# Attention times values with the values stationary in four column tiles, its result turned on VectorE, a job queue per engine and score steps in halves: a two-layer transformer on one core

## The chip, the cores and the metric

The kernel runs on one core of a Trainium2 chip. The metric is device time in microseconds of one execution of the whole program, as a median of several runs. Beside it there is one profiled execution, with its own time; the span in a profile runs from its first to its last instruction. TensorE (PE) multiplies matrices, with a row of its own for loading the stationary operand (PEld); VectorE (DVE), ScalarE (ACT) and GpSimd (POOL) work on elements; SyncE (SP) issues DMAs.

## The reference

Two layers, each an attention with a compressive memory (A) and a gated FFN (B), on 2,048 tokens of width 512; both layers use the same weights.

```python
x = x + A(layernorm(x)); x = x + B(layernorm(x))      # twice
# A: 32 heads of 16, 4 segments of 512 tokens, one after another
for s in range(4):
    logits = einsum('bhqd,bhkd->bhqk', qs, ks) * scale + mask      # causal inside the segment
    a_dot = einsum('bhqk,bhkd->bhqd', softmax(logits), vs)
    a_mem = (phi(qs) @ M) / (phi(qs) @ z + 1e-6)                   # phi(t) = t + 1 if t > 0 else exp(t)
    o = g * a_mem + (1 - g) * a_dot                                # g = sigmoid(beta), per head
    M, z = M + phi(ks)^T vs, z + sum(phi(ks))
# A ends in o @ wo;  B: (gelu(x @ w_gate) * (x @ w_up)) @ w_down, inner width 1792
```

## The kernel before

**Stages.** The work is 8 blocks k = 0..7 (layer k // 4, segment s = k % 4). Class `Att` makes for each block q, kf and kB transposed (feature b*128.. in partitions, token along the row), v by tokens (`vaug`: 16 columns a head and a 17th that holds 1 + exp(beta), so that one product gives numerator and denominator), scores, their product with v, and the memory's part (`mem_items`, `upd_item`). Class `Ffn` holds the output projection (`wo`), gate, up and down. kB is kf with every other head's 16 rows set to zero (`maskB`): a score matmul takes 16 rows of kf for even heads (par 0) or 32 rows of kB for odd ones.

**Scores.** A block has 20 score steps (`STEPS`): for each of four groups b of eight heads there are five steps, in which four row tiles of TensorE (32 rows each) write two PSUM tiles `st` of 128 keys x 1,024. ACT turns each into `pt` = exp(scale * st) by one instruction (L578), POOL zeroes the upper triangle of the diagonal blocks (`affine_select`, L592).

**Flush.** After steps 2 and 4 of a group the probabilities of four heads and all four key blocks are there and a flush follows: 64 in all. For each of 10 pairs of key block and query block and each head, pt (128 keys x 128 queries) is the stationary operand and 17 columns of vaug stream:

```python
nc.tensor.matmul(ps()[:, qi, j, :], lhsT=two[j // 2][:, j % 2, cb:cb + P],
                 rhs=self.vaug[:, ki, 8 * b + 2 * j + par, :], start=(c == 0), stop=(c == len(order) - 1))
```

That is 40 matmuls and 40 weight loads; the result `ps_q` has queries in partitions. DVE takes the reciprocal of the 17th column (L619) and multiplies (L628) into `ab`; behind the second flush of a group it adds the memory's part `am` (L644, blocks with s > 0), and a transposing DMA (`turn`, L215) makes aT, the stationary side of the output projection.

**Order.** Nothing runs by itself: Python plans the program with one clock per engine (`Clocks`) and writes each instruction into its engine's queue as the plan reaches it. The loop at the end follows TensorE's clock: a score step goes first when its operands and both `st` tiles are free, then the matmuls of the item that is open (an `Item`: a list of matmuls with a due time, one or more PSUM banks of four), then the ready item with the earliest due time; if a bank is free and nothing is ready, a filler matmul on a constant tile (`warm_ps`, L853). When an item's last matmul is planned, its function `done` writes the work of the other engines that follows at once: `evict` (L311 ff.) picks DVE or ACT by which clock would be done first, with `ACT_EVICT` in favour of DVE. The scheduled engines take their queues strictly in this order. kB is made by POOL (L382) behind the eviction of kf.

Of the kernel before, what the change touches and what calls it, by code (L numbers as in the profile page):

```python
# [21 lines left out]
NSEG = 4  # L22
L = 512
# [4 lines left out]
TPS = L // P  # L28
SCALE = DH ** -0.5
# [6 lines left out]
BY_PE = {("xnTf", 0), ("xnTf", 2 * NSEG - 1)}  # L36
# [7 lines left out]
ACT_EVICT = 0.5  # L44
FIRST_EVICT = 2.0


class Clocks:
# [5 lines left out]
    LATENCY = 0.055  # L54
    OVERLAP = {"act": 0.09, "dve": 0.07}

    def __init__(self):
        self.pe = self.act = self.dve = self.pool = self.sp = 0.0
        self.table = "exp"
        self.later, self.seq = [], 0  # L60
        self.ev = {}
# [8 lines left out]
    def run_due(self, t):  # L70
        while self.later and self.later[0][0] <= t:
            heapq.heappop(self.later)[2]()

    def run(self, engine, ready, *costs):

        for cost in costs:
            start = max(getattr(self, engine), ready + self.LATENCY)
            ready = start + cost
            setattr(self, engine, ready - self.OVERLAP.get(engine, 0.0))
        return ready  # L80

    def on_act(self, ready, cost, table=None):
        if table and table != self.table:
            self.act += 1.28
            self.table = table
        return self.run("act", ready, cost)
# [9 lines left out]

class Item:


    def __init__(self, due, ready, ops, done=None, banks=1, kind=""):  # L100
        self.due, self.ready, self.ops, self.done, self.banks, self.kind = due, ready, ops, done, banks, kind
# [3 lines left out]
def kernel(  # L105
# [56 lines left out]
    for h in range(2):  # L162
        pieces.append((64.0 + 5.0 * h, lambda h=h: load(
            wd_sb[:, 7 * h:7 * h + 7, :], B_w_down.rearrange("(ft p) n -> p ft n", p=P)[:, 7 * h:7 * h + 7, :])))
# [4 lines left out]
    warm_ps = psp.tile([P, L], F32, tag="m", bufs=M_BANKS)  # L169
# [26 lines left out]
    vaugs = [cst.tile([P, TPS, H, DH + 1], BF16, name=f"vaug{i}") for i in range(SETS)]  # L196
# [6 lines left out]
    def late_constants():  # L203
        for va in vaugs:
            nc.gpsimd.tensor_copy(out=va[:, :, :, DH], in_=cden[:].unsqueeze(1).to_broadcast([P, TPS, H]))
        for b in range(4):
# [5 lines left out]
    def turn_later(t, out, in_, landed):  # L212

        def go():
            nc.sync.dma_start_transpose(out=out, in_=in_)  # L215
            landed(ck.run("sp", t, 1.25) + 1.4)

        ck.at(t, go)


    class Norm:
        def __init__(self, key, tt0, bufs):
            self.key, self.tt0, self.bufs, self.mv = key, tt0, bufs, None
            self.n = 0

        def stats(self, j, ready):
            if self.mv is None:
                self.mv = wrk.tile([P, TPS, 2], F32, tag="bnmv", bufs=3)
            st6 = wrk.tile([P, 1, 6], F32, tag="bnst", bufs=4)
            nc.vector.bn_stats(out=st6[:, 0, :], in_=x_sb[:, self.tt0 + j, :])  # L230
            nc.vector.bn_aggr(out=self.mv[:, j, :], in_=st6[:])
            t = ck.run("dve", ready, 0.66, 0.17)
            self.n += 1
            if self.n == TPS:
                ck.at(t, lambda: self.scales(t))

        def scales(self, ready):
            ve = wrk.tile([P, TPS, 1], F32, tag="lnve")
            nc.gpsimd.tensor_scalar(out=ve[:], in0=self.mv[:, :, 1:2], scalar1=EPS_LN, scalar2=None, op0=ALU.add)
            self.rs = wrk.tile([P, TPS, 1], F32, tag="lnrs", bufs=3)  # L240
            nc.gpsimd.tensor_tensor(out=self.rs[:], in0=ve[:], in1=mhalf[:], op=ALU.pow)  # L241
            t = ck.run("pool", ready, 0.25, 1.05)
            if self.key in BY_PE:
                self.items_by_pe(t)
            else:
                ck.at(t, lambda: self.turned(t))

        def normed(self, j):
            xn = seg.tile([P, D], BF16, tag="xn", bufs=6)
# [4 lines left out]
        def turned(self, ready, j=0):  # L254
            if j == 0:
                self.xnT = seg.tile([P, KT, L], BF16, tag=self.key[0], bufs=self.bufs)
            xn = self.normed(j)
            t = ck.run("dve", ready, 0.333)

            def landed(t2):  # L260
                if j < TPS - 1:
                    self.turned(t, j + 1)
                else:
                    ev[self.key] = t2

            turn_later(t, self.xnT[:, :, j * P:(j + 1) * P], xn[:], landed)

        def items_by_pe(self, ready):
            self.xnT = seg.tile([P, KT, L], BF16, tag=self.key[0], bufs=self.bufs)
            left = [TPS]  # L270

            def item(j):
                xn = self.normed(j)
                t = ck.run("dve", ready, 0.333)
                ps = Box(lambda: psp.tile([P, KT, P], BF16, tag="m", bufs=M_BANKS, name="ps"))

                def done():
                    t2 = evict(self.xnT[:, :, j * P:(j + 1) * P], ps()[:])
                    left[0] -= 1
                    if not left[0]:  # L280
                        ev[self.key] = t2

                return Item(-0.5, lambda: t + Clocks.LATENCY <= ck.pe,
                            [(Clocks.MM[128], lambda kt=kt: nc.tensor.transpose(
                                ps()[:, kt, :], xn[:, kt * P:(kt + 1) * P], ident[:])) for kt in range(KT)],
                            done, kind="turn")

            ck.at(ready, lambda: items.extend([item(j) for j in range(TPS)]))

        def by_pe(self, j):  # L290
            xn = self.normed(j)
            ps = psp.tile([P, KT, P], BF16, tag="m", bufs=M_BANKS)
# [8 lines left out]

    banks = [0.0] * M_BANKS

    def product(name):
        return Box(lambda: psp.tile([P, L], F32, tag="m", bufs=M_BANKS, name=name))

    def free_bank(t):
        banks.append(t + 0.05)
        banks.sort()

    def evict(dst, src):  # L311
        ready = ck.made()
        on_dve = max(ck.dve, ready) + 0.67
        on_act = max(ck.act, ready) + 0.6
# [15 lines left out]
    class Box:  # L330
        def __init__(self, make):
            self.make, self.t = make, None
# [11 lines left out]
    class Att:  # L344
# [202 lines left out]
        def scores(self, t):  # L547
            k = self.k
            b, i = divmod(t, PAIRS)
            if i == 0:  # L550
                self.pts = {}
# [338 lines left out]
```

## Time and profile before

| | us |
|---|---|
| median of 3 runs | 599.21 (599.03 to 600.44) |
| the profiled execution's own time | 598.08 |
| its span | 596.2 |
| exponentials of scores, ACT, 320 | 310.1 |
| masks, POOL, 448 | 196.7 |
| gate, up and down matmuls, each 448 (busy time, overlapping) | 106.3, 102.6, 103.5 |

A line of a group reads: line, engine, operation, out<-in, shape, count, then busy time and mean duration in ns, then the idle time of the engine just ahead of them and what ended it. In the chain of waits, a piece has its start, its length and who ran. A window's row gives the busy time of PE, PEld, DVE, ACT and POOL, the granted clock (1.00 is full speed), the DMA share and GB/s. "issue" is idle time that no wait explains. Some matmul records are missing from the trace, so its counts can fall short of the program's.

### The profile page before, as it was taken

The numbers are of one execution on the slowest core, as the hardware profiler recorded it, in microseconds if no ns is written. First come the engines' busy times: TensorE is split into PE (matmuls) and PEld (weight loads), VectorE is DVE, ScalarE is ACT, GpSimd is POOL, SyncE is SP. The second block draws the span as 40 slices with busy tenths as digits, with TensorE's granted clock in tenths as the row PEclk, the third lists the DMA queues.
The fourth block names the chain that finished last, engine by engine and source line by source line (L and its number), as shares of the span: only waits on it lengthen the run. The fifth ranks groups of instructions, "written<-read, shape, count | busy, mean of one in ns | idle before, by whom it ended". The sixth has DMA issues, their size and how long they took to land.

```text
span 596.2 us, 14275 instructions
## 1 busy us (share of the span) xinstructions
PE 571.8 (96%) x5759; PEld 279.8 (47%) x5844; DVE 455.5 (76%) x921; ACT 415.2 (70%) x442; POOL 270.9 (45%) x527
## 2 busy tenths in 40 slices
PE   8898899999999999999999999999999999999997
PEld 3344444454445444444445455444454455444443
DVE  7889979776987777886677898789777885868161
ACT  2678779788868877897679957797478936770410
POOL 4777757433553356544546435553346424410000
PEclk9999979899999999999999999999999999999999
DMA  6178460200041002301230013200230003200001
GB/s 212 28 145 241 94 151 11 46 10 10 3 76 23 1 11 54 63 10 20 46 54 12 1 36 63 37 10 10 57 60 18 3 9 56 35 12 18 19 0 35
DMA packets 68513, 26.88 MB, mean 45 GB/s; under 512 B 59488, under 2 KB 67424, under 8 KB 68448
## 3 DMA queue, kind: packets, MB, share of 16 engines
q1 hardware_dynamic: 68304, 25.97, 20.5%
q8 instruction: 45, 0.74, 0.5%
q14 instruction: 20, 0.16, 0.1%
q10 hardware_dynamic: 144, 0.01, 0.0%
HBM read 9.71 MB, written 2.10 MB: 20 GB/s over the span
## 4 chain that ended last, share of the span: by engine, by line
PE 77%; DVE 13%; POOL 3%; issue 3%; ACT 2%; DMA 2%; ACTq 0%
PE psg L326 17%; PE psd L326 16%; PE psu L326 14%; PE ps_q L612 9%; PE st L571 7%; PE psqk L326 5%; PE pso L326 4%; PE psv L326 2%; DVE st L230 2%; POOL kB L382 2%; DVE xn L250 1%; PE warm_ps L853 1%; ACT pt L578 1%; DVE e L427 1%; POOL pt L592 1%
## 5 line engine op out<-in xcount | busy, mean ns | idle before, releaser
L578 ACT ACTIVATE pt<-st 128x1024 bf16<-128x1024 f32 x320 | 310.1, 1021 | 117.0 <-PE st L571 114.7
L592 POOL TENSOR_SCALAR_AFFINE_SELECT pt<-pt 128x256 bf16<-128x256 bf16 (+1 forms) x448 | 196.7, 459 | 214.6 <-ACT pt L578 208.0
L326 PE MATMUL psg<-xnT,wg_sb 128*128 128x512 bf16 x420 | 106.3, 382 | 3.3 <-DMA xnT<-xn 1.1
L326 PE MATMUL psd<-wd_sb,gel 128*128 128x512 bf16 x430 | 103.5, 380 | 2.0 <-DVE gel L705 0.9
L326 PE MATMUL psu<-xnT,wu_sb 128*128 128x512 bf16 x432 | 102.6, 379 | 0.8
L705 DVE TENSOR_TENSOR gel<-gel,psu 128x512 bf16<-128x512 bf16 x112 | 75.5, 685 | 31.2 <-PE psu L326 28.8
L612 PEld LDWEIGHTS <-pt 128*128 128x128 bf16 x2560 | 74.6, 96 | 21.1 <-issue 5.4
L612 PE MATMUL ps_q<-vaug,pt 128*128 128x17 bf16 x2560 | 76.3, 171 | 4.4 <-POOL pt L592 3.2
L319 DVE CAST gel<-psg 128x512 bf16<-128x512 f32 x96 | 64.8, 685 | 18.2 <-PE psg L326 17.0
L382 POOL TENSOR_SCALAR kB<-kf,maskB 128x512 bf16<-128x512 bf16 x32 | 50.5, 1579 | 35.3 <-DVE kf L319 31.6
L326 PEld LDWEIGHTS <-wu_sb 128*128 128x128 bf16 x448 | 41.8, 98 | 50.6 <-issue 4.3
L326 PEld LDWEIGHTS <-gel 128*128 128x128 bf16 x448 | 40.7, 98 | 51.2 <-issue 8.6
L326 PEld LDWEIGHTS <-wg_sb 128*128 128x128 bf16 x448 | 39.0, 98 | 49.0 <-issue 11.5
L719 DVE TENSOR_TENSOR x_sb<-x_sb,psd 128x512 bf16<-128x512 bf16 x32 | 21.9, 685 | 43.4 <-PE psd L326 43.4
L736 ACT ACTIVATE gel<-gel 128x2048 bf16<-128x2048 bf16 (+1 forms) x28 | 45.2, 1684 | 0.1
L230 DVE BATCH_NORM_STATS2 st<-x_sb 128x6 f32<-128x512 bf16 x60 | 41.4, 690 | 1.7
L571 PE MATMUL st<-q,kf 16*128 16x128 bf16 (+3 forms) x512 | 35.3, 306 | 1.1
L326 PE MATMUL psqk<-xnT,wq_sb 128*128 128x512 bf16 x123 | 34.7, 388 | 1.0 <-DVE xnT L297 0.6
L571 PE MATMUL st<-q,kB 32*128 32x384 bf16 (+3 forms) x512 | 34.5, 300 | 1.0
L326 PE MATMUL psqk<-xnT,wk_sb 128*128 128x512 bf16 x122 | 34.3, 388 | 0.5 <-issue 0.2
L326 PE MATMUL pso<-wo_sb,aT 128*128 128x512 bf16 x122 | 30.5, 379 | 0.8 <-DVE gel L705 0.4
L250 DVE TENSOR_SCALAR xn<-x_sb,mv,rs 128x512 bf16<-128x512 bf16 x64 | 29.7, 494 | 1.8 <-POOL rs L241 1.6
(82 smaller groups left out, 508.3 us busy)
## 6 DMA issues: line engine op xcount, KB each, us to landing
out_dram<-x_sb SPq DMA_DIRECT2D x16, 128.0 KB, 1.7
wg_sb<-in_B_w_gate_dram SPq DMA_DIRECT2D x4, 448.0 KB, 4.2
wu_sb<-in_B_w_up_dram SPq DMA_DIRECT2D x4, 448.0 KB, 6.5
wd_sb<-in_B_w_down_dram SPq DMA_DIRECT2D x2, 896.0 KB, 6.2
x_sb<-in_A_x_dram SPq DMA_DIRECT2D x3, 512.0 KB, 8.5
xnT<-xn SPq DMA_TRANSPOSE x52, 2.5
x_sb<-in_A_x_dram SPq DMA_DIRECT2D x4, 128.0 KB, 2.9
wq_sb<-in_A_wq_dram SPq DMA_DIRECT2D x1, 512.0 KB, 5.7
```

The lines of the kernel that those rows point to most:

```text
L230: nc.vector.bn_stats(out=st6[:, 0, :], in_=x_sb[:, self.tt0 + j, :])
L250: nc.vector.tensor_scalar(out=xn[:], in0=x_sb[:, self.tt0 + j, :], scalar1=self.mv[:, j, 0:1], scalar2=self.rs[:, j, :], op0=ALU.subtract, ...
L319: nc.vector.tensor_copy(out=dst, in_=src)
L326: return [(Clocks.MM[512], lambda i=i, l=l, r=r: nc.tensor.matmul(ps()[:], lhsT=l(), rhs=r(), start=(i == 0), stop=(i == n - 1))) for i, ( ...
L382: nc.gpsimd.tensor_scalar(out=self.kB[:, b, :], in0=self.kf[:, b, :], scalar1=maskB[:, 0:1], scalar2=None, op0=ALU.mult)
L571: nc.tensor.matmul(sts[j // 2][:, j % 2, c0:c0 + N], lhsT=lhsT[rows, b, P * ki:P * ki + P], rhs=self.q[rows, b, P * ki:L], start=True, sto ...
L578: nc.scalar.activation(out=pt[:], in_=st[:], func=ACT.Exp, scale=SCALE)
L592: nc.gpsimd.affine_select(out=dv, in_=dv, pattern=[[0, w], [1, P]], compare_op=ALU.is_ge, fill=0.0, base=0, channel_multiplier=-1)
L612: nc.tensor.matmul(ps()[:, qi, j, :], lhsT=two[j // 2][:, j % 2, cb:cb + P], rhs=self.vaug[:, ki, 8 * b + 2 * j + par, :], start=(c == 0), ...
L705: nc.vector.tensor_tensor(out=g, in0=g, in1=ps()[:], op=ALU.mult)
L719: nc.vector.tensor_tensor(out=xt, in0=xt, in1=ps()[:], op=ALU.add)
L736: nc.scalar.activation(out=g, in_=g, func=ACT.Gelu_apprx_tanh)
```

## The change

1. **Flush.** vaug is now the stationary operand: for each key block, 32 columns of vaug (a head's 17 and the 15 that follow, which nothing reads) in each of four column tiles, one a head, and the probabilities of all later queries stream (512, 384, 256 or 128 columns). 16 matmuls in place of 40. The result has head j in partitions 32j.., with queries along the row.
2. **Turn.** DVE transposes that tile in blocks of 32x32 into `byq` (f32, SBUF), takes reciprocal and product as before into `ab`, and behind the second flush transposes `ab` in 32x32 blocks into aT. The memory's part goes through the transposing DMA instead (`amT`) and is added to aT.
3. **Job queues.** Each engine has a queue of jobs (`Engine`), with a time from which a job may start and a slack; `serve` writes the job whose time plus slack is lowest. An eviction is posted to DVE and ACT at once, and whichever comes to it first takes it. Buffers are named one by one (`m0` to `m3`, `xn0` to `xn3`, `st0`, `st1`) instead of taken from rotating pools.
4. **Half steps.** A score step can be issued as two halves with two row tiles and one `st` tile each, where TensorE has nothing else to do. A flush that is ready goes right behind a score step.
5. kB is made by DVE; the w_down loads come later and in four pieces; POOL also zeroes the 15 columns behind vaug's last head.

```diff
+class Engine:
+    def serve(self, now):
...
+        start = max(self.free, min(j[0] for j in self.jobs) + self.LATENCY)
+        if start > now:
+            return False
+        job = min((j for j in self.jobs if j[0] + self.LATENCY <= start + 0.03), key=lambda j: j[0] + j[1])
...
-    for h in range(2):
-        pieces.append((64.0 + 5.0 * h, lambda h=h: load(
...
+    for h in range(4):
+        r = slice(FT * h // 4, FT * (h + 1) // 4)
+        pieces.append((94.0 + 3.2 * h, lambda r=r: load(
...
-                nc.gpsimd.tensor_scalar(out=self.kB[:, b, :], in0=self.kf[:, b, :], scalar1=maskB[:, 0:1],
-                                        scalar2=None, op0=ALU.mult)
...
+                    ck.dve.post(t, NORMAL, (0.285, lambda: nc.vector.tensor_scalar(
+                        out=self.kB[:, b, :], in0=self.kf[:, b, :], scalar1=maskB[:, 0:1], scalar2=None,
+                        op0=ALU.mult), lambda t2: ev.update({("kB", k, b): t2})))
...
-        def scores(self, t):
+        def scores(self, t, halves):
...
-                for j in range(4):
+                for j in [2 * n + m for n in halves for m in range(2)]:
...
         def flush_item(self, b, par, pts, masked):
             k = self.k
-            ps = Box(lambda: psp.tile([P, TPS, 4, DH + 1], F32, tag="m", bufs=M_BANKS, name="ps_q"))
...
-                nc.tensor.matmul(ps()[:, qi, j, :], lhsT=two[j // 2][:, j % 2, cb:cb + P],
-                                 rhs=self.vaug[:, ki, 8 * b + 2 * j + par, :], start=(c == 0),
-                                 stop=(c == len(order) - 1))
+            ps = Psum()
+            order = (0, 1, 3, 2) if par == 0 else (0, 2, 1, 3)
...
+                for n, ki in enumerate(order):
+                    two, c0 = pts[par, ki]
+                    for j in range(4):
+                        h = 8 * b + 2 * j + par
+                        nc.tensor.matmul(ps()[32 * j:32 * j + 32, P * ki:L],
+                                         lhsT=self.vaug[:, ki, h * (DH + 1):h * (DH + 1) + 32],
+                                         rhs=two[j // 2][:, j % 2, c0:c0 + L - P * ki], start=(n == 0), stop=(n == 3),
+                                         tile_position=(0, 32 * j))
...
+                def turn():
+                    made["byq"] = byq = wrk.tile([P, TPS * 4, 32], F32, tag="byq", bufs=1, name="byq")
+                    nc.vector.transpose(out=byq[:].rearrange("p a c -> p (a c)"), in_=ps()[:])
...
+                def back():
...
+                    nc.vector.transpose(out=self.aT[:, b, :], in_=self.ab[b][:].rearrange("p a c -> p (a c)"))
+
+                def add():
+                    nc.vector.tensor_tensor(out=self.aT[:, b, :], in0=self.aT[:, b, :], in1=self.amT[b][:], op=ALU.add)
...
+                ck.dve.post(ck.made(), SOON, (0.673, turn, ps.read), (0.251, inverse, None),
+                            (0.417, scale, kept if par else None))
...
+        free = [f <= ck.pe - 0.05 for f in st_free]
+        if half:
+            return (1,) if free[1] else ()
+        return (0, 1) if all(free) else (0,) if free[0] and idle else ()
```

TensorE's queue around the first flush (block 0; `st` are scores, `warm` fillers, `pt` probabilities). Before, the end of the fifth score step, fillers, and the flush's first pair:

```order
L571 MATMUL st<-q,kB 128x128
L853 LDWEIGHTS warm
L853 MATMUL warm_ps<-warm 128x512
L853 LDWEIGHTS warm
L853 MATMUL warm_ps<-warm 128x512
L612 LDWEIGHTS pt
L612 MATMUL ps_q<-vaug_131,pt 128x17
```

And with the change (`m` is a PSUM bank):

```order
L1044 LDWEIGHTS warm
L1044 MATMUL m<-warm 128x512
L710 LDWEIGHTS kB
L710 MATMUL st<-q,kB 128x384
L710 LDWEIGHTS kB
L710 MATMUL st<-q,kB 128x384
L710 LDWEIGHTS kB
L710 MATMUL st<-q,kB 128x128
L710 LDWEIGHTS kB
L710 MATMUL st<-q,kB 128x128
L756 LDWEIGHTS vaug_131
L756 MATMUL m<-pt,vaug_131 32x512
```

Of the fifth score step only one half (two row tiles) stands ahead of the flush, and its other half behind; the flush holds vaug and streams pt in 32 rows of output.

DVE's queue over the first two flushes of block 0 (`st_` are statistics of the next norm, `xn` its normalized rows). Before:

```order
L619 RECIPROCAL r<-ps_q 128x16
L628 TENSOR_TENSOR ab<-ps_q,r 128x16x16
L619 RECIPROCAL r<-ps_q 128x16
L628 TENSOR_TENSOR ab<-ps_q,r 128x16x16
L250 TENSOR_SCALAR xn<-x_sb,mv,rs 128x512
L425 TENSOR_SCALAR e<-e 128x512
L427 SCALAR_TENSOR_TENSOR e,zk<-kf,e 128x512
```

With the change:

```order
L769 STREAM_TRANSPOSE byq<-m 128x512
L773 RECIPROCAL r<-byq 128x16
L778 TENSOR_TENSOR ab<-byq,r 128x16x16
L784 STREAM_TRANSPOSE aT<-ab 128x512
L339 CAST kf<-m 128x512
L395 TENSOR_SCALAR xn<-x_sb,mv,rs 128x512 x4
L486 TENSOR_SCALAR kB<-kf,maskB 128x512 x2
L555 TENSOR_SCALAR e<-e 128x512
L541 SCALAR_TENSOR_TENSOR e,zk<-kf,e 128x512
```

The second flush of the group is followed by two transposes in place of one DMA, and two kB multiplications that POOL did stand between xn and the next phi.

More of the change, by code (lines that the diff above doesn't have):

```diff
@@ L22 @@
 NSEG = 4
+NK = 2 * NSEG
 L = 512
@@ L68, in at, with when, serve, busy @@
         heapq.heappush(self.later, (t, self.seq, fn))
[L70 to L86, printed above, removed]
+    def when(self, cond, fn):
+        if cond():
+            fn()
+        else:
+            self.waiting.append((cond, fn))
+    def serve(self):
+        again = True
+        while again:
+            again = False
+            while self.later and self.later[0][0] <= self.pe:
+                heapq.heappop(self.later)[2]()
+                again = True
+            for w in list(self.waiting):
+                if w[0]():
+                    self.waiting.remove(w)
+                    w[1]()
+                    again = True
+            first = min(self.engines, key=lambda e: max(e.free, min((j[0] for j in e.jobs), default=1e9)))
+            again |= first.serve(self.pe) or any(e.serve(self.pe) for e in self.engines)
+    def busy(self):
+        return self.later or self.waiting or any(e.jobs for e in self.engines)
     def made(self):
@@ new lines, in evict, with end, dense @@
+    def evict(ps, dst, src, told, slack=NORMAL):
+        taken = []
+        def end(t):
+            ps.read(t)
+            told(t)
+        first = FIRST_EVICT if ("scores", 0) not in ev else ACT_EVICT
+        ck.dve.post(ck.made(), slack, (0.673, lambda: nc.vector.tensor_copy(out=dst(), in_=src()), end), taken=taken)
+        ck.act.post(ck.made(), slack + first, (0.602, lambda: nc.scalar.activation(
+            out=dst(), in_=src(), func=ACT.Copy), end), taken=taken)
+    def dense(ps, pairs):
+        n = len(pairs)
+        return [(Clocks.MM[512], lambda i=i, l=l, r=r: nc.tensor.matmul(ps()[:], lhsT=l(), rhs=r(), start=(i == 0),
+                                                                        stop=(i == n - 1)))
+                for i, (l, r) in enumerate(pairs)]
@@ new lines, with next_e @@
+    streams = [(k, t) for k in range(NK) for t in range(STEPS)]
+    opened, half = None, 0
+    def next_e():
+        if not e_slots.free or e_slots.queue:
+            return
+        now = streams[0][0] + streams[0][1] / STEPS if streams else 1e9
+        act = ck.act
+        idle = act.free <= ck.pe and act.table == "exp" and not any(j[0] <= ck.pe and not j[4] for j in act.jobs)
+        got = [j for j in e_jobs if j[1] <= ck.pe and j[2]() and (idle or j[0] <= now)]
+        if got:
+            job = min(got, key=lambda j: j[0])
+            e_jobs.remove(job)
+            job[3](job[1], E_SLACK)
+            ck.serve()
@@ new lines, in score_now, with open_item @@
+    def score_now(idle=False):
+        if not streams or not (step_free or half):
+            return ()
+        k, t = streams[0]
+        if not att[k].score_ready(t):
+            return ()
+        free = [f <= ck.pe - 0.05 for f in st_free]
+        if half:
+            return (1,) if free[1] else ()
+        return (0, 1) if all(free) else (0,) if free[0] and idle else ()
+    def open_item(got):
+        it = min(got, key=lambda it: it.due)
+        items.remove(it)
+        it.ps.bank = min((i for i in range(M_BANKS)), key=lambda i: banks[i])
+        banks[it.ps.bank] = 1e9
+        return it
@@ new lines, in score @@
+    def score(halves):
+        k, t = streams[0]
+        att[k].scores(t, halves)
+        if halves[-1]:
+            streams.pop(0)
+        got = [it for it in items if it.kind == "flush" and it.ready()]
+        if got and min(banks) <= ck.pe:
+            it = open_item(got)
+            it.ops[0][1]()
+            ck.on_pe(it.ops[0][0] - Clocks.SWITCH)
+            it.done()
+        return 1 - halves[-1]
+    while streams or items or opened or ck.busy():
+        ck.serve()
+        next_e()
+        halves = score_now()
+        if halves:
+            half = score(halves)
```

753 lines of the change are left out of this document (396 added, 357 removed).

## The prediction

> **What bounds the kernel now.** I read the page first: busy shares, the slices, the chain of waits.
>
> ```profile
> span 596.2 us, 14275 instructions
> PE 571.8 (96%) x5759; PEld 279.8 (47%) x5844; DVE 455.5 (76%) x921; ACT 415.2 (70%) x442; POOL 270.9 (45%) x527
> PEclk9999979899999999999999999999999999999999
> PE 77%; DVE 13%; POOL 3%; issue 3%; ACT 2%; DMA 2%; ACTq 0%
> ```
>
> The reader is to see that TensorE is busy in 96% of the span at full clock, except for two slices early on, and that 77% of the chain that ended last is TensorE itself. DVE has 24% idle, ACT 30%. So time is TensorE's queue, and a change is worth what it takes out of that queue, unless another engine makes TensorE wait. A busy PE row overlaps its neighbour, so I price TensorE from start to start, in the chain of waits and in the timeline of stage 218 to 232 us:
>
> ```profile
> 546.25 4.53 PE psd L326 x21
> 592.77 0.69 DVE x_sb L719
> 222.98 2.11 PE L326 MATMUL psd<-wd_sb,gel 128*128 128x512 bf16 x9 [0.16 <-issue]
> 225.02 0.40 PE L571 MATMUL st<-q,kB 32*128 32x512 bf16 x4
> 225.35 0.82 PE L326 MATMUL psd<-wd_sb,gel 128*128 128x512 bf16 x3
> 226.01 1.15 PE L612 MATMUL ps_q<-vaug,pt 128*128 128x17 bf16 x40
> 227.01 0.81 PE L326 MATMUL psd<-wd_sb,gel 128*128 128x512 bf16 x2
> ```
>
> A dense matmul of 512 columns costs 4.53 / 21 = 0.216 us. Nine of them from 222.98 end their turn at 224.92; the score step begins at 225.02 and the next dense matmul at 225.35. A **score step** thus costs 0.43: 0.10 to enter, 0.216 for four row tiles of 512 columns that stream together, 0.11 to leave. A **flush** (40 matmuls of 17 columns, in the whole array) costs 227.01 - 226.01 = 1.00, nothing to enter or leave.
>
> Only the first 105 us are not like this. The first q matmul and the first gate matmul in the timeline, and the busy time by stretches of 20 us (PE, PEld, DVE, ACT, POOL, clock):
>
> ```profile
> 10.39 1.02 PE L326 MATMUL psqk<-xnT,wq_sb 128*128 128x512 bf16 x4 [0.61 <-DVE xnT L297]
> 105.81 0.61 PE L326 MATMUL psg<-xnT,wg_sb 128*128 128x512 bf16 x1
> 40.00:60.00 20.00, 17.94 (x200) 9.08 (x200) 19.02 (x43) 16.02 (x20) 15.85 (x24) 1.00 0.77 222
> 60.00:80.00 20.00, 17.23 (x221) 8.43 (x222) 16.04 (x38) 14.66 (x19) 12.24 (x24) 0.79 0.61 137
> 80.00:100.00 20.00, 19.67 (x212) 9.58 (x214) 18.43 (x41) 16.60 (x22) 12.74 (x22) 0.95 0.26 53
> 540.00:560.00 20.00, 19.74 (x102) 9.47 (x104) 11.42 (x23) 2.91 (x6) 1.27 (x2) 1.00 0.08 26
> 560.00:580.00 20.00, 19.95 (x93) 9.10 (x93) 8.36 (x13) 6.54 (x11) 0.00 (x0) 1.00 0.00 1
> 580.00:600.00 20.00, 12.63 (x58) 5.56 (x57) 4.02 (x6) 0.00 (x0) 0.00 (x0) 0.97 0.08 26
> ```
>
> TensorE's order before the first gate matmul holds 208 dense matmuls (44.9), 31 score steps (13.3), 11 flushes (11.0), 30 fillers (6.5) and 100 small ones (68 of 128 columns, 32 of 8, at a quarter and an eighth of 0.216: 4.6); with 10.4 ahead of them that is 90.7. The gate came at 105.8: **15 us of waiting and of slow clock** in the start. There DVE is busy 18 or 19 of 20 us. The end, by the same sum, loses only some 10 us more in the 487 us that follow.
>
> **The change part by part.** The groups whose counts change:
>
> ```profile
> L612 PE MATMUL ps_q<-vaug,pt 128*128 128x17 bf16 x2560 | 76.3, 171 | 4.4 <-POOL pt L592 3.2
> L853 PE MATMUL warm_ps<-warm 128*128 128x512 bf16 x49 | 16.0, 419 | 1.0 <-DVE vaug L319 0.6 <-DVE am L475 0.2
> L319 DVE CAST gel<-psg 128x512 bf16<-128x512 f32 x96 | 64.8, 685 | 18.2 <-PE psg L326 17.0
> L425 DVE TENSOR_SCALAR e<-e 128x512 bf16<-128x512 bf16 x48 | 16.3, 341 | 1.7 <-ACT e L421 1.6
> L427 DVE SCALAR_TENSOR_TENSOR e<-kf,e 128x512 bf16<-128x512 bf16 x24 | 17.9, 746 | 0.8
> L382 POOL TENSOR_SCALAR kB<-kf,maskB 128x512 bf16<-128x512 bf16 x32 | 50.5, 1579 | 35.3 <-DVE kf L319 31.6
> L316 ACT ACTIVATE kf<-psqk 128x512 bf16<-128x512 f32 x4 | 2.4, 598 | 0.4 <-PE psqk L326 0.4
> ```
>
> *Flushes.* There are 64. Each becomes 16 matmuls: for four key blocks of 512, 384, 256 and 128 columns, four column tiles side by side. If the four stream together, as the four row tiles of a score step do, that is 1,280 columns at 0.216 / 512, or 0.54, with 0.10 to enter and 0.11 to leave: 0.75. 64 x (0.75 - 1.00) = **-16.0**. No row shows column tiles; the bounds are 0.54 (no entry, no exit) and 0.75 + 0.40, where weights are not hidden (rival A). I take 0.75, since entry and exit are measured on the nearest row.
>
> *Neighbours.* In the new order 12 flushes stand right behind a score step and 16 right ahead of one; there one entry and exit are shared instead of two: 28 x -0.10 = **-2.8** (bounds 0 and -2.8).
>
> *Half steps.* 20 of the 160 score steps are issued as two halves with two row tiles each. A half streams the same columns, so it costs a whole 0.43 more: 20 x 0.43 = **+8.6**. They stand among fillers, where TensorE has nothing else; the fillers rise from 49 to 58: 9 x 0.216 = **+1.9**. Half steps and fillers are idle time made visible: the faster flushes leave TensorE ahead of ACT in the early stages.
>
> *What DVE takes over.* 64 turns of a 128x512 f32 tile out of PSUM, 32 turns of a 128x512 bf16 tile, 32 kB multiplications. DVE rows with 512 elements in a partition lie between 0.341 (bf16, one source) and 0.746; a turn reads PSUM like the cast, so I take 0.685. kB is like the row at 0.341. 96 x 0.685 + 32 x 0.341 = 76.7. The order hands 58 evictions from DVE to ACT (gate 35, k 9, v 8, q 6): -58 x 0.685 = -39.7. DVE: 455.5 + 37 = 492.5, of some 585 us 84%. ACT takes 58 x 0.60 = 35 and stands at 450, 77%. POOL loses all 50.5 of kB. The bank of a flush is held as long as before (0.685, against reciprocal 0.25 and product 0.42). All this lies beside TensorE, as long as DVE's queue doesn't grow: its cover is the 24% idle. If it is gone, each turn shows (rival B).
>
> Bounds for a turn: 0.341 below; above, two passes over the tile, 1.37. The page "VectorE: DVE Perf Modes" of the Trainium skill (The three transpose paths) gives 311 ns for a 128x128 bf16 turn in 32x32 blocks; with 384 more elements at its 0.96 GHz an estimate is 0.71, by which the DVE sum would be 2 us higher and the time the same.
>
> *Transposing DMAs.* 32 DMAs of ab become 24 of am, which has long been there when it is needed; output projection no longer waits for a DMA behind the last flush. No row of the waits names an output projection that waited for it, so I count 0 there. The loads of w_down go out later in four pieces; their first use is 30 us and more behind, also 0.
>
> *Start.* In the new order 85.2 us of TensorE stand before the first gate matmul (208 dense 44.9, 34 score steps 14.6, 10 flushes 7.5, 26 fillers 5.6, small ones 2.2, and 10.4). kB, on the chain in this stage, goes from 1.58 to about 0.34:
>
> ```profile
> 17.48 1.57 POOL kB L382
> 19.77 1.54 POOL kB L382
> 35.33 1.79 POOL kB L382
> 38.43 1.54 POOL kB L382
> ```
>
> ACT now has 58 exponentials at 1.02, 11 of phi at 0.63 and 30 evictions and copies at 0.60 ahead of the first gate eviction, 84 us behind the 9.8 at which it starts, some less since neighbours overlap. So the gate can hardly come before 90; I expect 97, a loss of 12 in place of 15: **-3**. The bounds are -10 (ACT packed) and +3 (as much lost as before, and DVE's turns in front).
>
> **Sum**, against the profiled execution's own 598.1 (span 596.2): -16.0 - 2.8 + 8.6 + 1.9 - 3 = -11.3, so 586.8. The median before, 599.21, lies 1.1 above that execution: **588**.
>
> **The rivals.**
>
> *A: weights of the column tiles aren't hidden (slower).* A flush loads 16 sets of weights. Where a set must wait for the stream ahead of it, four loads show at each of four key blocks. Rows of a score step, loads and matmuls:
>
> ```profile
> 222.42 0.10 PEld L571 LDWEIGHTS <-kf 16*128 16x128 bf16 x4 [0.23 <-issue]
> 222.43 0.29 PE L571 MATMUL st<-q,kf 16*128 16x256 bf16 x4
> 222.44 0.10 PEld L571 LDWEIGHTS <-kB 32*128 32x128 bf16 x4
> 222.55 0.28 PE L571 MATMUL st<-q,kB 32*128 32x256 bf16 x4
> ...
> L326 PEld LDWEIGHTS <-gel 128*128 128x128 bf16 x448 | 40.7, 98 | 51.2 <-issue 8.6
> ```
>
> Four loads take 0.10, so the price is 4 x 0.10 = 0.40 a flush: 64 x 0.40 = +25.6, or 613. It turns slower from 0.18 a flush on. Against it: kB's loads lie inside the stream of kf's matmuls on the same rows. The page "TensorE: Matmul & The Clock Gate" of the Trainium skill (Part 3, The mechanism) says that loads overlap running matmuls only where the row group differs, and all column tiles share the row groups; by that rule this rival would be the forecast. The rows above speak against the rule, and so do the loads of gel, 0.098 each on all rows of the array, which fit into the 0.216 rhythm of the dense matmuls. Chance 8%.
>
> *B: a turn takes two passes (slower).* 96 x 0.685 = +66, so DVE has 558 to do; with the 32 us that it can't use at the end (11.4, 8.4 and 4.0 busy from 540 to 596) and 8 at the start it can't end before 598, with waits about 606. Chance 9%.
>
> *C: more gain.* The start packs against ACT (-7 more) and entry and exit of a flush overlap (0.65, -6): 575. Chance 10%.
>
> *D: no change.* DVE at 84%, one queue in order, answers later; TensorE waits for banks:
>
> ```profile
> PE ps_q L612 <- POOL pt L592: 3.2, 7, 0.8
> PE psg L326 <- DVE am L475: 0.4, 1, 0.4
> ```
>
> Such waits are small now. 0.17 us at each of 64 flushes returns it all: 597 to 601. Chance 10%.
>
> *E: the column tiles run one behind another,* so the change doesn't do what it says: 4 x 0.54 + 0.21 = 2.37 a flush, +104 on the sum, 692. The four row tiles, together in 0.40, speak against it. Chance 3%.
>
> **How the numbers follow.** The forecast itself (578 to 597) has 60%. 574 to 604 leaves out the lower part of C (4%), A, E and half of B, some 19%. What a measurement of this kernel can tell from no change is 0.3%, 1.8 us. Faster: the forecast, C, and a little of D, 0.72; the same, 0.09; slower: A, B, E, the edge of D, and of the start's loss, 0.19.
>
> **What would show it.** In the profile after: from a flush's first matmul to the next dense one 0.65 (with 0.10 ahead of it); 16 loads inside the flush without a gap; turns at 0.69; DVE near 490, ACT near 450, POOL near 220 busy; the first gate matmul near 97; no PE wait of over 5 us in total on DVE. The forecast is wrong if flushes cost 0.93 or more, if turns are 1.0 or more, or if TensorE's rows show new idle on DVE or ACT.

## The result, and the profile after

| | before | changed |
|---|---|---|
| median, measured side by side | 599.83 us (599.03 to 601.18, 4 runs) | 582.81 us (581.52 to 585.5, 4 runs) |
| the profiled execution's own time | 598.08 | 584.07 |
| its span | 596.2 | 582.4 |

The ratio is 0.972, with a 95% interval of 0.9675 to 0.9765: 17 us faster. The forecast was 588, so the sign and the range held and the point was 5 us too high.

The page of the changed kernel: its span, busy times, the granted clock in 40 slices, and the engines' shares of the chain of waits.

```profile
span 582.4 us, 11265 instructions
PE 559.6 (96%) x4240; PEld 234.2 (40%) x4317; DVE 484.5 (83%) x991; ACT 441.7 (76%) x500; POOL 226.0 (39%) x498
PEclk8999999999999999999999999999999999999999
PE 75%; DVE 16%; DMA 3%; issue 3%; ACT 2%; POOL 0%; POOLq 0%; another core or an unknown queue 0%; DVEq 0%; ACTq 0%
```

TensorE is as busy as before (96%) in a span 13.8 us shorter: it still bounds, and what went is work in its queue and the gaps of the start. DVE has 29 us more to do, ACT 26 more, POOL 45 less.

The timeline of TensorE in the same stage as before (start, length, instruction, count, in brackets the idle time ahead), first a flush that adjoins a score step, then one between dense matmuls:

```profile
207.67 2.33 PE L345 MATMUL m<-wd_sb,gel 128*128 128x512 bf16 x10
209.93 0.40 PE L710 MATMUL st<-q,kf 16*128 16x384 bf16 x8
210.26 0.73 PE L756 MATMUL m<-pt,vaug 128*32 128x512 bf16 x16
210.92 1.69 PE L345 MATMUL m<-wd_sb,gel 128*128 128x512 bf16 x6
...
234.78 1.47 PE L345 MATMUL m<-xnT,wg_sb 128*128 128x512 bf16 x6
236.18 0.73 PE L756 MATMUL m<-pt,vaug 128*32 128x512 bf16 x16
236.84 0.39 PE L345 MATMUL m<-xnT,wg_sb 128*128 128x512 bf16 x1
```

The second: six dense matmuls from 234.78 end their turn at 234.78 + 6 x 0.216 = 236.08; the flush begins 0.10 to 0.11 later and the next dense matmul 0.66 after that. A flush alone is **0.77**, where it was 1.00. The first: ten dense matmuls end at 209.83 and the next begins at 210.92, so a score step and a flush side by side take 1.09, where apart they take 0.43 + 0.77 = 1.20: one exit and entry are shared, worth 0.11.

The groups that are new or grew (out<-in, shape, count, busy us, mean ns, idle ahead and what ended it):

```profile
L769 DVE STREAM_TRANSPOSE byq<-m 128x512 f32<-128x512 f32 x64 | 45.3, 707 | 11.2 <-PE m L756 10.8
L784 DVE STREAM_TRANSPOSE aT<-ab 128x512 bf16<-128x512 bf16 x32 | 22.6, 706 | 0.6
L486 DVE TENSOR_SCALAR kB<-kf,maskB 128x512 bf16<-128x512 bf16 x32 | 11.6, 369 | 0.7 <-ACT kf L340 0.5
L340 ACT ACTIVATE gel<-m 128x512 bf16<-128x512 f32 x37 | 21.7, 603 | 21.2 <-PE m L345 20.4
```

A turn takes 0.707 whether it is f32 out of PSUM or bf16 out of SBUF, and ACT now evicts 37 gate tiles, where it evicted 2.

The start, by the timeline and by stretches of 20 us (PE, PEld, DVE, ACT, POOL, clock), and TensorE's longest waits and the last eviction:

```profile
10.81 1.59 PE L345 MATMUL m<-xnT,wq_sb 128*128 128x512 bf16 x4 [0.61 <-DVE xnT L431]
90.08 1.89 PE L345 MATMUL m<-xnT,wg_sb 128*128 128x512 bf16 x7
578.84 0.69 DVE L820 TENSOR_TENSOR x_sb<-x_sb,m 128x512 bf16<-128x512 bf16 x1 [2.33 <-PE m L345]
```

```profile
0.00:20.00 20.00, 16.18 (x77) 6.56 (x79) 13.05 (x35) 8.03 (x13) 8.11 (x25) 0.91 0.48 158
40.00:60.00 20.00, 19.47 (x171) 7.98 (x173) 18.98 (x48) 18.91 (x26) 9.32 (x21) 1.00 0.69 182
60.00:80.00 20.00, 19.70 (x158) 7.23 (x164) 16.00 (x34) 18.82 (x24) 10.77 (x23) 1.00 0.27 83
```

```profile
PE m L345 <- issue: 3.3, 21, 0.2
PE st L710 <- ACT pt L738: 3.1, 8, 0.6
PE m L345 <- DVE am L600: 2.3, 2, 1.8
```

The first gate matmul comes at 90.1 in place of 105.8. In the start, from 40 to 80 us, ACT is busy 18.9 us of 20 where it was 14.7 to 16.0, and TensorE 19.5 and 19.7 where it was 17.9 and 17.2. The clock was 0.79 from 60 to 80 us before; here it is full there and 0.91 in the first 20.

**Where the 14 us came from.** Price TensorE's order by the rows: 0.216 a dense matmul, 0.43 a score step or a half, 1.00 or 0.77 a flush, 0.10 less for each adjoining pair, and 10.4 ahead of them. That is the time TensorE would need if nothing made it wait at full clock. The difference to the start of the last eviction is waiting and slow clock, and the first gate matmul cuts it into two parts.

| us | before | changed | difference |
|---|---|---|---|
| queue of TensorE by row prices | 569.2 | 562.3 | -6.9 |
| waits and slow clock up to the first gate matmul | 15.1 | 5.3 | -9.8 |
| waits and slow clock behind it | 8.5 | 11.2 | +2.7 |
| start of the last eviction | 592.8 | 578.8 | -14.0 |

Of the start's 9.8, the clock is a part: before, 20 x 0.21 + 20 x 0.05 = 5 us of it by the granted clock of 60 to 100 us, and now 20 x 0.09 = 2. Another execution of the changed kernel, at full clock in the start, had its first gate matmul at 88.28, so the dip did cost about 2. Right behind its first gate matmul the kernel before had one more dip (0.91 from 100 to 120 us, 20 x 0.09 = 2) and the changed kernel had none behind its own, so the waits alone grew there by more than the 2.7, by some 4.4 us.

### The profile page after: what moved, and what is told of

It reads as the page before. It is cut to its first block, busy times and chain, and to the rows that moved or that the text cites. A ratio compares the mean times of both kernels' runs of the same rounds, so it can differ in the third digit from the quotient of the medians.

```text
span 582.4 us, 11265 instructions
## 1 busy us (share of the span) xinstructions
PE 559.6 (96%) x4240; PEld 234.2 (40%) x4317; DVE 484.5 (83%) x991; ACT 441.7 (76%) x500; POOL 226.0 (39%) x498
## 4 chain that ended last, share of the span: by engine, by line
PE 75%; DVE 16%; DMA 3%; issue 3%; ACT 2%; POOL 0%; POOLq 0%; another core or an unknown queue 0%; DVEq 0%; ACTq 0%
PE m L345 59%; PE st L710 7%; PE m L756 5%; PE m L1044 2%; DVE gel L873 2%; ACT pt L738 2%; DVE x_sb L820 2%; DVE xn L395 2%; DMA amT<-am 1%; DVE st L365 1%; DVE byq L769 1%; DVE aT L784 1%; DMA xnT<-xn 1%; DVE e L541 1%; DVE phiq L541 1%
## 5 line engine op out<-in xcount | busy, mean ns | idle before, releaser
L345 PE MATMUL m<-xnT,wg_sb 128*128 128x512 bf16 x425 | 106.5, 380 | 4.9 <-DVE am L600 2.3
L345 PE MATMUL m<-xnT,wu_sb 128*128 128x512 bf16 x431 | 102.6, 380 | 1.5 <-issue 0.8
L345 PE MATMUL m<-wd_sb,gel 128*128 128x512 bf16 x430 | 102.4, 380 | 1.4 <-issue 0.8
L873 DVE TENSOR_TENSOR gel<-gel,m 128x512 bf16<-128x512 bf16 x112 | 73.9, 683 | 21.7 <-PE m L345 20.9
L820 DVE TENSOR_TENSOR x_sb<-x_sb,m 128x512 bf16<-128x512 bf16 x64 | 42.6, 676 | 27.1 <-PE m L345 25.7
L769 DVE STREAM_TRANSPOSE byq<-m 128x512 f32<-128x512 f32 x64 | 45.3, 707 | 11.2 <-PE m L756 10.8
L339 DVE CAST gel<-m 128x512 bf16<-128x512 f32 x61 | 41.2, 684 | 9.8 <-PE m L345 8.3
L756 PE MATMUL m<-pt,vaug 128*32 128x512 bf16 (+3 forms) x1024 | 46.6, 302 | 0.0
L710 PE MATMUL st<-q,kf 16*128 16x384 bf16 (+3 forms) x512 | 40.1, 302 | 2.0 <-ACT pt L738 1.4
L345 PE MATMUL m<-xnT,wq_sb 128*128 128x512 bf16 x125 | 34.9, 388 | 1.6 <-DMA xnT<-xn 0.7
```

What stands on the lines that cost most here:

```text
L339: ck.dve.post(ck.made(), slack, (0.673, lambda: nc.vector.tensor_copy(out=dst(), in_=src()), end), taken=taken)
L345: return [(Clocks.MM[512], lambda i=i, l=l, r=r: nc.tensor.matmul(ps()[:], lhsT=l(), rhs=r(), start=(i == 0), stop=(i == n - 1))) for i, ( ...
L710: nc.tensor.matmul(sts[j // 2][:, j % 2, c0:c0 + N], lhsT=lhsT[rows, b, P * ki:P * ki + P], rhs=self.q[rows, b, P * ki:L], start=True, sto ...
L756: nc.tensor.matmul(ps()[32 * j:32 * j + 32, P * ki:L], lhsT=self.vaug[:, ki, h * (DH + 1):h * (DH + 1) + 32], rhs=two[j // 2][:, j % 2, c0 ...
L769: nc.vector.transpose(out=byq[:].rearrange("p a c -> p (a c)"), in_=ps()[:])
L820: ck.dve.post(ck.made(), slack, (0.683, lambda: nc.vector.tensor_tensor(out=xt, in0=xt, in1=ps()[:], op=ALU.add), lambda t: (ps.read(t), t ...
```

## The experiments

Two theories. **T1**: each part pays what the prediction gave it, above all the flush on TensorE's queue, -0.23 x 64. **T2**: the flush alone pays little, because the other engines do not keep up; the queues of jobs are needed to turn the shorter queue of TensorE into time, by handing evictions to ACT. All runs but the three of the warmer start are in one table. A ratio is to the kernel before, run beside it on the same chip, where its median was 597.7 to 599.8, so ratios compare better than medians. The column of ACT has the evictions it takes, by the rows of the groups; the last three are as in the table above, worked out for each from the order and the timeline of one execution:

| run | median, us | ratio (95%) | ACT evicts | fillers | queue | lost in the start | lost behind |
|---|---|---|---|---|---|---|---|
| before | 599.83 | 1 | 30 | 49 | 569.2 | 15.1 | 8.5 |
| changed | 582.81 | 0.972 (0.9675-0.9765) | 88 | 58 | 562.3 | 5.3 | 11.2 |
| e1 changed, old flush | 595.61 | 0.9972 (0.994-1.0005) | 66 | 41 | 572.2 | 8.4 | 10.7 |
| e2 before, new flush | 593.67 | 0.9936 (0.9898-0.9973) | 65 | 82 | 560.5 | 12.7 | 14.3 |
| e3 before, kB on DVE | 596.27 | 0.9965 (0.9947-0.9982) | 33 | 44 | 568.2 | 13.8 | 9.7 |
| e7 before, new flush, kB on DVE | 605.87 | 1.0123 (1.0098-1.0149) | 76 | 118 | 568.0 | 13.5 | 16.5 |
| e10 e7 with more to ACT | 607.88 | 1.0168 (1.0147-1.019) | 124 | 125 | 569.6 | 9.5 | 22.9 |
| e4 changed, no halves | 583.45 | 0.9774 (0.9727-0.9821) | 98 | 82 | 560.2 | 5.4 | 11.5 |
| e5 changed, kB on POOL | 583.29 | 0.9743 (0.9695-0.9791) | 84 | 42 | 559.1 | 8.4 | 12.0 |
| e6 changed, turn twice | 601.65 | 1.0053 (1.0025-1.0081) | 110 | 54 | 559.6 | 4.2 | 30.3 |
| e8 changed, DVE evicts in the start | 597.06 | 0.9969 (0.9944-0.9994) | 72 | 21 | 552.7 | 26.0 | 13.4 |

**The old flush in the new queues.** The flush goes back to 40 matmuls with pt stationary, reciprocal and product read PSUM, and ab goes through a transposing DMA; the queues, half steps and kB stay as changed.

```diff
-                    for j in range(4):
-                        nc.tensor.matmul(ps()[32 * j:32 * j + 32, P * ki:L], ..., tile_position=(0, 32 * j))
+                    nc.tensor.matmul(ps()[:, qi, j, :], lhsT=two[j // 2][:, j % 2, cb:cb + P],
+                                     rhs=by_head(self.vaug)[:, ki, 8 * b + 2 * j + par, :], start=(n == 0),
...
-                    steps = [(0.673, back, None if self.s else there)]
+                    turn_later(ck.pe, SOON, dst, lambda: self.ab[b][:].rearrange("p t d -> p (t d)"), landed)
```

> The changed kernel with the flush of before: probabilities stationary, 40 matmuls of 17 columns at 1.00 each, no 32x32 turns, a transposing DMA to aT; job queues, half steps and kB on VectorE stay. Theory 1 (the flush is what gains): 64 x 0.23 = 15 us come back, 597 to 599. Theory 2 (the job queues and kB make the start shorter, 10 us, and the flush only adds to that): about 590, with the first gate matmul still near 90 to 93. If both hold, DVE relief of 68 us adds nothing.

595.61: everything but the flush and its turn is worth 2.7 us, and its interval reaches just past 1. This lies between the two times expected: the queues and kB did not bring 10 us by themselves, and the first gate matmul came at 96.5, not at 90 to 93. The run brings a burden of its own: DVE waits 14.9 us in all for the DMA to aT before it adds the memory's part, though TensorE's waits for DVE sum to only 3.4.

**The new flush in the old order.** The kernel before with the new flush and its turns alone (kB stays on POOL). To fit, xn has five buffers in place of six, ab and am two, and the memory's mask is bf16.

```diff
-                nc.tensor.matmul(ps()[:, qi, j, :], lhsT=two[j // 2][:, j % 2, cb:cb + P],
-                                 rhs=self.vaug[:, ki, 8 * b + 2 * j + par, :], start=(c == 0),
+                        nc.tensor.matmul(ps()[32 * j:32 * j + 32, P * ki:L],
+                                         lhsT=self.vaug[:, ki, h * (DH + 1):h * (DH + 1) + 32],
...
+                nc.vector.transpose(out=byq[:].rearrange("p a c -> p (a c)"), in_=ps()[:])
...
+            nc.vector.transpose(out=self.aT[:, b, :], in_=self.ab[b][:].rearrange("p a c -> p (a c)"))
```

> The kernel of before with only the flush changed: column tiles, turns on VectorE, memory part through the transposing DMA; its own planner, whole score steps, kB on GpSimd. To fit memory xn has 5 buffers instead of 6, ab and am 2 instead of 4, bdg is bf16. Theory 1: 599.8 - 15 = 585 with the start as before (first gate near 106). Theory 2: the start, where VectorE was 95% busy, grows by the turns there (12 x 0.7 = 8 us), so 590 to 596.

593.67: alone the flush is worth 0.64%, some 4 us beside the kernel before on the same chip, though 64 of them take 0.23 less each. The table says where it went: 33 more fillers (+7 us of queue), and 3.4 us more waits and slow clock. Stretches of this run:

```profile
20.00:40.00 20.00, 18.85 (x139) 6.86 (x137) 18.07 (x39) 15.08 (x19) 16.62 (x28) 1.00 0.35 85
40.00:60.00 20.00, 18.26 (x154) 7.57 (x153) 19.52 (x46) 16.06 (x21) 15.35 (x23) 1.00 0.91 234
60.00:80.00 20.00, 17.23 (x167) 7.08 (x165) 18.52 (x38) 16.12 (x20) 16.02 (x28) 1.00 0.44 99
```

DVE is at 18 to 19.5 us of 20 while ACT is at 15 to 16: the evictions stand on the engine that is full. The first two runs make a square: the flush gives 0.6% under the old order and 2.5% under the new one, the rest of the change 0.3% with the old flush and 2.2% with the new. T1 falls: the parts do not add.

Two things are mixed into these shares. One is the granted clock: it was 0.989 in the mean of the 20 executions of the kernel before beside these runs, 0.997 in the five of e2, 0.990 in the ten of e1, and 0.998 in the eight of the changed kernel. Over 590 us, 0.008 is some 5 us: as much as e2 gains at all, and 5 of the 13 us between e1 and the change. The other is the smaller buffers of e2: with two of them for am, DVE waits 6.8 us in all for the DMAs that read them, and the kernel before has no such wait. No run has the new flush in the old order with the old buffers, so what they cost there is open.

**kB alone.** The kernel before with kB's multiplication on DVE.

```diff
-                nc.gpsimd.tensor_scalar(out=self.kB[:, b, :], in0=self.kf[:, b, :], scalar1=maskB[:, 0:1],
+                nc.vector.tensor_scalar(out=self.kB[:, b, :], in0=self.kf[:, b, :], scalar1=maskB[:, 0:1],
...
-                ev["kB", k, b] = ck.run("pool", t, 0.635)
+                ev["kB", k, b] = ck.run("dve", t, 0.285)
```

> The kernel of before with kB made by VectorE (0.34) instead of GpSimd (1.58), nothing else. If kB on the chain of the start is what cost 10 us there, 590 to 594 with the first gate matmul near 97. If not, 598 to 601.

596.27: 2 us in the kernel before, its interval clear of 1, between the two times expected. And the other way round, the changed kernel with kB on POOL:

```diff
-                    ck.dve.post(t, NORMAL, (0.285, lambda: nc.vector.tensor_scalar(
+                    ck.pool.post(t, NORMAL, (0.635, lambda: nc.gpsimd.tensor_scalar(
```

> The changed kernel with kB made by GpSimd again (planned at 0.635 as in the kernel before, where it took 1.58). If the move of kB to VectorE is what shortens the start here, the first gate matmul goes from 90 to 97 and the time from 582.8 to 588 to 592. If it is worth what it was worth in the old planner (2 us), 583 to 586.

583.29, where the interval covers the change's own ratio: in the new order the move is worth nothing that shows. With POOL the start loses 3 us more (8.4 against 5.3), but 16 fillers fewer pay it back.

**Half steps away.**

```diff
-        return (0, 1) if all(free) else (0,) if free[0] and idle else ()
+        return (0, 1) if all(free) else ()
```

> The changed kernel without half steps. If half steps are only idle time made visible, 582 to 584. If they feed ScalarE earlier and so shorten the start, 586 to 590. If they cost their 20 x 0.43 us, 575.

583.45, and a ratio whose interval overlaps the change's own (0.9774, 0.9727 to 0.9821, against 0.972): not told apart. 20 extra halves (8.6 us) become 24 more fillers (5.2), and the queue by row prices is 2 us shorter with no gain. So halves and fillers look like the same idle time under two names.

**What DVE's cover is worth.** Each f32 turn is done twice (the second writes the same again), 45 us more for DVE.

```diff
-                ck.dve.post(ck.made(), SOON, (0.673, turn, ps.read), (0.251, inverse, None),
+                ck.dve.post(ck.made(), SOON, (0.673, turn, None), (0.673, turn, ps.read), (0.251, inverse, None),
```

> The changed kernel with each 32x32 turn out of PSUM made twice (64 more of 0.71 on VectorE, 45 us; the second writes the same again), planned as such; ScalarE then takes 110 evictions instead of 88. Theory 1 (VectorE's 17% idle covers the turns): 583 to 588. Rival (VectorE sets the time already, so that the turns are paid in full): 605 and more.

601.65, 19 us more, between the two times expected. The busy times of this run, the engines' shares of its chain of waits, and TensorE's longest waits for ACT and for DVE:

```profile
PE 566.6 (95%) x4238; PEld 235.7 (39%) x4313; DVE 518.0 (87%) x1033; ACT 451.7 (76%) x522; POOL 230.1 (38%) x498
PE 63%; DVE 25%; ACT 5%; issue 4%; DMA 2%; POOL 1%; ACTq 0%; DVEq 0%
```

```profile
PE st L710 <- ACT pt L738: 6.3, 15, 0.7
PE m L345 <- DVE gel L873: 2.1, 4, 0.7
```

DVE stands at 87%, and its share of the chain goes from 16 to 25%, though no single wait is long. The start is untouched (4.2 lost); the loss behind it goes from 11.2 to 30.3. Some 3 or 4 us of that are clock (0.991 the median of these runs, 0.994 to 1.0 in those of the changed kernel, over 600 us). TensorE's waits for DVE sum to 11.1 us (6.7 in the changed kernel), and its longest row is for ACT's exponentials, 6.3 in place of 3.1: ACT took 22 evictions more in this run. So DVE's idle share is not free to spend: 45 us of work cost 19. How they cost it is shown in part only. TensorE's waits of all rows together are 7 us longer than in the changed kernel, which with the clock makes some 10 of the 19. And the second turn also holds the flush's bank 0.7 us longer, which no run separates from DVE's load.

**Who evicts in the start.** In the changed kernel evictions go to DVE alone until the first output projection is planned.

```diff
-        ck.act.post(ck.made(), slack + first, (0.602, lambda: nc.scalar.activation(
-            out=dst(), in_=src(), func=ACT.Copy), end), taken=taken)
+        if ("wo", 0) in ev:
+            ck.act.post(ck.made(), slack + first, (0.602, lambda: nc.scalar.activation(
+                out=dst(), in_=src(), func=ACT.Copy), end), taken=taken)
```

> The changed kernel where evictions can go to ScalarE only after the first output projection; before that VectorE makes them all. Its TensorE queue is 10 us shorter by row prices (21 fillers instead of 58). If ScalarE's share of the evictions is what shortens the start, the first gate matmul moves from 90 to 97 or later and the time to 588 to 592. If the start is bound by ScalarE's exponentials, the first gate comes at 88 to 90 and the time is 578 to 582.

597.06, beyond the 588 to 592 expected: 16 evictions fewer on ACT, and nearly all of the gain is gone, although TensorE's queue is 10 us shorter by row prices (21 fillers). Its stretches and its first gate matmul:

```profile
40.00:60.00 20.00, 17.21 (x149) 7.30 (x156) 19.55 (x42) 16.58 (x20) 8.88 (x21) 1.00 0.76 208
60.00:80.00 20.00, 14.23 (x139) 4.94 (x130) 19.55 (x47) 16.41 (x19) 12.47 (x24) 0.81 0.25 43
80.00:100.00 20.00, 17.07 (x147) 6.40 (x146) 16.33 (x36) 15.40 (x18) 9.56 (x22) 0.76 0.14 29
108.03 1.03 PE L346 MATMUL m<-xnT,wg_sb 128*128 128x512 bf16 x4
```

DVE is full (19.55 of 20), TensorE starves, and the granted clock falls to 0.81 and 0.76 as well. The start loses 26 us in place of 5; by the granted clock of 60 to 120 us (0.81, 0.76 and 0.92) some 10 of the 26 are slow clock, the rest waits. ACT's help there is needed.

**Is it enough?** The old order once more, with new flush and kB on DVE (the edits of the second and third run together), and the same with the thresholds at which its planner gives an eviction to ACT lowered.

```diff
-ACT_EVICT = 0.5
-FIRST_EVICT = 2.0
+ACT_EVICT = -0.5
+FIRST_EVICT = 0.0
```

> The kernel before with the new flush (as in the run with the flush alone, 593.7) and with the kB multiplication on VectorE besides; its planner and its order of issue stay the old ones. If the parts of the change add, this is the flush alone plus the 2 us that the kB move gave alone: about 592, ratio 0.990. If instead the old planner turns what it is given into fillers, as it did with the flush alone, its TensorE queue decides: by the row prices it is 568.0 us against 560.5 with the flush alone (118 fillers against 82), and the time is 596 to 600, ratio near 1.0, with VectorE over 500 us busy.

> As the run beside it (old planner, new flush, kB on VectorE), but the planner's two thresholds for giving an eviction to ACT are lowered (2.0 to 0.0 in the start, 0.5 to -0.5 behind it), so that ACT takes some 30 evictions more and VectorE as many fewer. If the queues of the change bring their gain by handing evictions to ACT, this recovers much of it: start loss below 8 us, time 583 to 590, at least 6 us under the run beside it, though its TensorE queue by row prices is 569.6 (1.6 us more). If the order in which TensorE's jobs are taken is what brings it, the time stays within 3 us of the run beside it.

605.87, beyond the 596 to 600 expected, and 607.88: with everything that the change moves to DVE, the old order is slower than the kernel before. It is not the queue: by row prices e7's is 1.2 us shorter than that of the kernel before, in spite of 118 fillers, and 6.4 us more are lost to waits and slow clock. Handing 48 evictions more to ACT (30 were expected) does what T2 says in the start (9.5 lost against 13.5), and gives it all back behind it. T2's second half falls: ACT's share is needed, but not enough. The waits of the two (engine, instruction, what it waited for: us, times, longest), e7 first:

```profile
DVE am L480 <- DMA amT<-am: 8.5, 6, 3.7
PE psg L331 <- DVE byq L632: 3.3, 2, 2.6
PE psqk L331 <- DVE am L480: 2.2, 1, 2.2
PE ps_q L624 <- DVE am L480: 2.1, 3, 1.5
```

```profile
DVE am L480 <- DMA amT<-am: 12.0, 9, 2.8
DVE aT L658 <- DMA amT<-am: 6.8, 1, 6.8
PE pso L331 <- DVE am L480: 3.0, 1, 3.0
PE ps_q L624 <- DVE am L480: 2.9, 3, 2.0
```

In the order that is written once and for all, DVE stands up to 6.8 us before a product or a sum of the memory's part, for a DMA that reads the buffer or brings the other operand, with turns and evictions behind it in its queue; TensorE then waits for these. Summed over their rows, TensorE waits 20.9 and 19.5 us for DVE here, 6.7 in the changed kernel and 7.2 before. The changed kernel has the same two buffers for am, and DVE waits 1.9 us in all for those DMAs. That the queues pay because a job waits outside DVE's instruction stream until its operand is there agrees with these rows; no run separates it from the different choice of TensorE's next item, so this stays open.

**A warmer start.** Four more matmuls on the constant tile ahead of the first q matmul (23 in place of 19), against the dip of the clock in the first 20 us; run twice, the second time beside the changed kernel.

```diff
-WARM = 19
+WARM = 23
```

> The changed kernel with 23 instead of 19 warming matmuls ahead of the first transposes. If the slow clock of the first 20 us (0.91 in the profile of the changed kernel, 1.00 in two of its other runs, which were 3 us faster) comes from TensorE's idle time at 7 us, the clock stays at 1.00 and the median falls by 1 to 2 us, to 581; if not, 583.

> The changed kernel itself, once more, beside the run with four more warming matmuls: 581.5 to 585.5 by its four runs so far, ratio 0.972.

> The changed kernel with WARM 23 instead of 19 again: if the clock's dip in the first 20 us (0.91 granted in the profiled run of the changed kernel, 1.00 with 23) is what spreads its runs, the slow ones near 585 are gone here and the median is 1 to 2 us under the changed kernel's on the same chip; if the dip comes whatever stands ahead of it, both medians agree within 1 us.

581.89 (ratio 0.9722, 0.9665 to 0.9779) the first time; side by side 582.24 (0.974, 0.9722 to 0.9758) for the changed kernel and 581.20 (0.9729, 0.971 to 0.9748) with 23. Both times 1 us under the changed kernel, and both intervals overlap: not told apart. The runs near 585 didn't come back in either kernel, so they say nothing for the four matmuls. It is the fastest version here, by a margin that isn't shown.

## Why the prediction was right

- **TensorE bounds: right.** It is at 96% before and after, and 75% of the chain.
- **The flush: right,** 0.77 against 0.75, so 64 x -0.23 = -14.7 against -16.0; the changed kernel with the old flush (e1) is 13 us slower, some 5 of it clock. The four column tiles stream together and rivals A and E fall: 1,280 columns with 16 loads among them take 0.66, of which 0.54 is the stream. Had a set of weights waited for the stream ahead of it, the flush would have stood at 1.15. The rule from "TensorE: Matmul & The Clock Gate" of the Trainium skill (Part 3, The mechanism), that loads overlap running matmuls only where the row group differs, does not hold here: all 16 loads use all rows, and none shows.
- **Neighbours: right.** 0.11 for a pair, against 0.10.
- **Half steps and fillers: counted right** (+8.6 and +1.9 stand in the queue's -6.9), and they look like idle time, as the prediction said: without halves the time could not be told apart.
- **DVE, ACT, POOL: right in size.** 484.5, 441.7 and 226.0 busy, against 490, 450 and 220; a turn 0.707 against 0.685, so rival B's two passes fall. The estimate worked out from "VectorE: DVE Perf Modes" of the Trainium skill (The three transpose paths), 0.71, is met.
- **The cover was judged too kindly.** "All this lies beside TensorE, as long as DVE's queue doesn't grow" holds for the changed kernel, but the reason given, 24% idle, does not carry it. At 87% busy (e6) 19 of 45 us show. Under the old order, with its smaller buffers, the same turns and kB cost more than the flushes save (e7). What hid them lies, as far as these runs go, in the new order, and the prediction had no term for it; which part of that order does it stays open. Rival D's mechanism shows in e7, where TensorE waits 20.9 us for DVE; in the changed kernel it did not strike.
- **The start: the term that was mis-sized.** -3 forecast (a loss of 12 in place of 15, the gate at 97), -9.8 measured (5.3, the gate at 90.1). This was rival C's first half, ACT packed, which had its row: ACT's work ahead of the gate was put at 84 us behind 9.8, less overlaps, and it did nearly pack so, at 18 to 19 us busy of each 20. Its second half, a flush of 0.65, did not come. A further part of the -9.8 is clock: TensorE lost about 5 us to slow clock in the start before and 2 after, which the sum had in its loss of 15 but took for given. That the shorter start needs ACT's share of the evictions is shown by e8, which takes it away.
- **Behind the start** 2.7 us more are lost than before, for which the sum had no term; no single wait shows it (the longest row on DVE is 2.3 in total, as the prediction wanted, and all its rows sum to 6.7, where they were 7.2).

So -11.3 against -14.0 on the profiled execution: the queue -6.9 against -8.3, the start -9.8 against -3, and +2.7 behind it. The queue misses by 1.4 and the stretch behind the start by 2.7 one way, the start by 6.8 the other. That the total came within 3 us is in part luck: errors of opposite sign met.

## What to carry to other kernels

Taking 15 us out of the queue of the bounding engine paid 4 us where the order around it stayed, and 13 where that order was remade, with some 5 us of faster clock in each: in these runs time saved turned into fillers unless the engines beside TensorE delivered earlier, so look in each stage at what feeds TensorE next, and not at an engine's idle share over the span. An engine at 76 to 83% in one strictly ordered queue had little cover here; double its new work in an experiment before calling it hidden. When moving work between engines, test the parts crossed with the order that carries them, since single parts (0.6%, 0.3%) may say little of both together (2.8%).

## What the runs showed of the hardware

- The way in and out of a tiled stretch costs 0.10 and 0.11 us for row tiles and for column tiles alike, and is paid once where the two kinds adjoin.
- A turn in 32x32 blocks of 128x512 takes as long in bf16 out of SBUF (706 ns) as in f32 out of PSUM (707 ns).
- The granted clock is in part the kernel's own doing. It dips in stretches in which TensorE starves (0.81 and 0.76 with TensorE 14.2 and 17.1 us busy of 20 in e8), though not in every one (e2 had 17.2 of 20 at full clock). Its mean over an execution was 0.980 to 0.994 in all of the kernel before that are on record, 0.994 to 1.0 in the eight of the changed one and 0.979 to 0.983 in the ten of e8; 0.009 between the means of the first two (0.989 and 0.998) is some 5 of the 17 us. So a wait in the start can cost more than its length. What sets a dip off was not tried.
- A dip is a stretch at half clock, and its length comes in steps. Asked for by itself, the row of the kernel before gives 0.50 from 71.62 to 81.86 us and 1.00 on either side; the changed kernel has 0.50 from 11.13 to 14.53 us, and e8 from 72.32 to 89.37. That is 10.2, 3.4 and 17.1 us, or three, one and five times 3.4, and one step costs 1.7 us. The means of executions fall in the same steps, of about 0.003 (1.000, 0.997, 0.994, 0.991), which over 590 us is 1.8. The page "TensorE: Matmul & The Clock Gate" of the Trainium skill (Part 1, The HAM clock gate) says that the clock is halved after an idle window of about 3.4 us, and is full again after a busy one. These traces agree with the length and with the half, but TensorE was not idle ahead of the three dips: it was busy 1.84, 1.80 and 1.98 us of the 3.4 before them. In the second run with 23 warming matmuls (e12), a stretch with 1.61 busy of 3.4 (226.2 to 229.6 us) brought no dip.
